# Eight half passes in a slot instead of four, tails moved to other products, and fewer small steps around them

## The chip, the cores and the metric

The kernel runs on one core of a Trainium2 chip. The time is the device time of one execution in microseconds (us). Three runs of the kernel before took 1652.21 us (median; 1650.31 to 1655.63).

## The reference

`x` is 2048 rows of 576 values. The kernel computes `x + s * g`, where both branches start from the same normed rows.

```python
xn = layernorm(x)                                    # [2048, 576]
# s: attention, 32 heads of 18, each row sees itself and the 255 rows before it
q, k, v = split(xn @ wqkv)                           # wqkv [576, 1728]
p = softmax(where(mask, q @ k.T * 18 ** -0.5, -1e9))
s = (p @ v) @ wo                                     # wo [576, 576]
# g: two branches multiplied, no nonlinearity between them
h = (xn @ w_gate) * (xn @ w_up)                      # [2048, 4608]
g = silu(h @ w_down)                                 # w_down [4608, 576]
out = x + s * g
```

## The kernel before

**Precision.** Every matrix is held as a sum of two f16 parts, a high one and a low one (what the rounding of the first left over). A product of two such matrices is three matmuls: high with high, high with low, low with high. One matmul of 128 rows of the contraction by 128 by 256 columns is called a pass here.

**Tiling of the gate and up products.** 4608 columns are worked off in 18 groups of 256 (`g`), 2048 rows of `x` in 4 chunks of 512 (`c`): 72 slots, and slot `sl` is group `sl // 4`, chunk `sl % 4`. In a slot the product of a 512-wide weight block (576 = 512 + 64 rows) with 512 rows of `x` is made by a seven-product scheme on 2 by 2 blocks: seven products `q` = 0 to 6 on sums and differences of blocks, in the order 0, 2, 1, 3, 4, 5, 6. Each has 12 passes (two kinds, gate and up; two blocks of 128; three part products). The differences of weights (`tw`) are formed per group by `t_sum`, `t_hi`, `t_lo`, the sums of `x` (`sx`, `xd`) once ahead.

**The last 64 rows.** 576 is not a multiple of 128: 64 rows are left. A tail is their product. A full tail pass carries 64 rows of two parts at once; what is left over is a half pass, a matmul with 64 rows of contraction, which uses half of the array's rows. In the kernel before, products 1, 4, 5 and 6 have tails: 1 and 6 with two full passes a kind, 4 and 5 with one full and one half (`seven_tail`, `seven_half`). A slot has 96 full passes and four half passes; the half passes stand together at place 11, those of product 4 on rows 0 to 63 of the array and those of 5 on rows 64 to 127, alternating.

**Banks.** The seven products use two PSUM banks (`up`, 512 columns: gate and up side by side). `ON` says which product accumulates on the bank of which: 1 on 0, 3 on 2, 5 on 3, 6 on 4. A product that goes on a bank that was already read out must wait for that reading. Readings (`seven_read`): product 0 and 1 by ScalarE (`seven_copy`), the others by VectorE (`seven_add`, one PSUM and one SBUF input), into f32 tiles `gt`. When a quarter is complete, `seven_mult` multiplies gate by up into `ht`; `h_hi` (ScalarE) and `h_lo` (VectorE) split that into two f16 parts `hh`.

**Down projection.** `down` n = 0 to 4 runs in the next slot: six passes of 512 columns each (n = 4: 24 passes of 64 columns) into one bank `dn`, and VectorE adds it to `acc`. The next `down` waits for that.

**Attention.** One step of two heads by 512 rows in each of slots 1 to 64: scores on TensorE (`score_pairs`, matmuls of 54 rows in pairs on the two halves of the array), masked row maximum on VectorE (`score`), exponent on ScalarE (`probs`), low part by a subtraction (`turn_probs`), then a DMA transpose into `pt`, then `weigh` on TensorE into `pv`; `finish` divides by the sum and adds the two parts, `finish2` splits the result.

**Order.** All is written out by hand: a slot has 16 places, `SEVEN_N` says how many passes each place issues, and the table `AT` gives the place of everything else (place 22 of a slot is place 6 of the next). At a place the passes come first, then scores, then `down`, then the rest. Each engine takes its instructions in this order; all DMAs go through the SP queue. Per group there is also the scaling of new weights: `ffn_raw` loads them, `ffn_amax` squares and sums, the maxima go out to DRAM and back (`ffn_spread_out`, `ffn_spread_in`), `ffn_scale` makes the powers of two on VectorE, `ffn_scale2` on GpSimd, then `up_hi`, `up_lo`, `dn_hi`, `dn_lo` split the weights.

Line numbers of the profile: L1116 full passes, L1072 and L1074 half passes, L991 `down`, L998 its addition, L908 `weigh`, L864 scores, L875 score reading, L1088 `seven_add`, L1084 `seven_copy`, L1094 `seven_mult`, L970 `h_hi`, L975 `h_lo`, L919 to L923 `finish`, L936 and L937 `finish2`, L896 `turn_probs`, L430 to L433 with L157 to L161 `ffn_scale`, L472 `t_sum`, L512 sums of `x`.

## Time and profile before

| what | value |
|---|---|
| median of 3 runs | 1652.21 us (1650.31 to 1655.63) |
| profiled execution, its own time | 1657.39 us |
| its span, first to last instruction | 1655.5 us |
| mean granted TensorE clock | 0.993 |
| busy: PE, DVE, ACT, POOL | 96%, 82%, 63%, 47% |
| first and last half pass | 191.1 us and 1582.6 us |

PE is TensorE's matmuls, PEld its weight loads, DVE is VectorE, ACT ScalarE, POOL GpSimd, SP the engine whose queue issues the DMAs. A row of the groups gives line, engine, operation, output and inputs, shapes and count, then busy us and mean ns of one, then the idle time before it and what ended that. Before 179 us lie the norm and the q, k, v products; slots 0 to 71 run from there to about 1588 us; the output projection ends the program. Matmuls are pipelined: the duration of one (some 270 ns) is longer than the distance to the next, so what a pass costs is read from the distance of starts.

### The profile page before, as it was taken

The page shows a single profiled execution, that of the slowest core. Times are in us where ns is not written, and L with a number is a line of the kernel's source. Part 1 is how long each engine was busy: PE and PEld are TensorE (multiplying, and loading weights), DVE is VectorE, ACT ScalarE, POOL GpSimd, SP SyncE. Part 2 cuts the span into 40 slices and gives each one's busy share as a digit, 9 for nine tenths or more (in the row PEclk, how much of TensorE's full clock was granted, in tenths as well). Part 3 has the DMA queues.
Part 4 walks back from the last instruction along what each step waited for, and adds up shares of the span by engine and source line. Part 5 has one row for each costly group of instructions (what it writes and reads, how often), then busy time and mean ns, then how long its engine had stood idle before and what let it go on. Part 6 is the DMA issues. An engine that isn't in the chain of part 4 may idle for free.

```text
span 1655.5 us, 40444 instructions
## 1 busy us (share of the span) xinstructions
PE 1584.0 (96%) x15498; PEld 1122.7 (68%) x15498; DVE 1353.2 (82%) x3049; ACT 1042.3 (63%) x1781; POOL 784.0 (47%) x993
## 2 busy tenths in 40 slices
PE   8999899999999999999999999999999999999898
PEld 5464566777766767676766666766676676677677
DVE  7536897989898979898988989898989797977654
ACT  6434566676677767777767676767777676752130
POOL 3125454546454746465655656464746473631000
PEclk9999999999999999999999999999999999999999
DMA  9562346475646777767868686768686868641228
GB/s 240 159 183 107 106 83 126 87 129 90 128 100 131 131 121 134 138 138 118 148 110 150 113 147 110 147 120 146 112 148 113 146 110 145 112 89 37 60 68 219
DMA packets 565745, 206.92 MB, mean 125 GB/s; under 512 B 506288, under 2 KB 546352, under 8 KB 565552
## 3 DMA queue, kind: packets, MB, share of 16 engines
q1 hardware_dynamic: 565552, 204.35, 63.9%
q8 instruction: 121, 1.98, 0.5%
q14 instruction: 72, 0.59, 0.1%
HBM read 76.63 MB, written 23.75 MB: 61 GB/s over the span
## 4 chain that ended last, share of the span: by engine, by line
PE 56%; DVE 23%; DMA 8%; issue 4%; SPq 4%; POOL 3%; ACT 1%; DVEq 0%; ACTq 0%; POOLq 0%
PE up L1116 23%; PE dn L991 14%; DMA pt<-pp 6%; PE s L373 3%; DVE gt L1088 3%; PE pv L908 3%; DVE acc L998 3%; DVE ht L1094 2%; DVE upw L185 2%; PE s L991 2%; DVE hh L975 2%; PE s L1223 2%; PE s L864 1%; PE up L1223 1%; PE up L373 1%
## 5 line engine op out<-in xcount | busy, mean ns | idle before, releaser
L991 PE MATMUL dn<-dnw,hh 128*128 128x512 f16 (+1 forms) x3168 | 448.9, 287 | 21.4 <-DVE acc L998 10.6
L1116 PEld LDWEIGHTS <-tw 128*128 128x128 f16 x3456 | 329.5, 98 | 78.0 <-issue 13.3
L991 PEld LDWEIGHTS <-hh 128*128 128x128 f16 x3456 | 224.6, 98 | 198.8 <-issue 37.6
L1116 PEld LDWEIGHTS <-upw 128*128 128x128 f16 x3456 | 322.6, 97 | 52.0 <-issue 0.4
L1116 PE MATMUL up<-XT,upw 128*128 128x256 f16 x2304 | 330.2, 272 | 0.0
L998 DVE SCALAR_TENSOR_TENSOR acc<-dn,sc,acc 128x512 f32<-128x512 f32 x310 | 214.7, 693 | 115.5 <-PE dn L991 110.2
L1088 DVE SCALAR_TENSOR_TENSOR gt<-up,gt 128x512 f32<-128x512 f32 x360 | 246.6, 685 | 31.5 <-PE up L1116 16.9
L1116 PE MATMUL up<-XT,tw 128*128 128x256 f16 x1728 | 237.4, 275 | 11.4 <-DVE gt L1088 11.4
L883 ACT ACTIVATE mx<-mx,sig 128x2 f32<-128x2 f32 x256 | 97.8, 382 | 218.7 <-DVE mx L875 218.7
L1116 PE MATMUL up<-sx,tw 128*128 128x256 f16 x1728 | 224.6, 273 | 0.4 <-DVE gt L1088 0.4
L908 PEld LDWEIGHTS <-pt 128*128 128x128 f16 x2880 | 107.8, 96 | 71.5 <-DMA pt<-pp 33.1
L970 ACT ACTIVATE hh<-ht 128x512 f16<-128x512 f32 x144 | 90.0, 625 | 91.0 <-DVE ht L1094 87.9
L908 PE MATMUL pv<-vt,pt 128*128 128x37 f16 x2880 | 123.8, 179 | 24.3 <-DMA pt<-pp 24.1
L1094 DVE TENSOR_TENSOR ht<-gt 128x256 f32<-128x256 f32 x288 | 147.0, 530 | 0.0
L1084 ACT ACTIVATE gt<-up 128x512 f32<-128x512 f32 x144 | 84.1, 584 | 56.5 <-PE up L1116 56.3
L1116 PE MATMUL up<-sx,upw 128*128 128x256 f16 x864 | 117.7, 273 | 0.0
L975 DVE SCALAR_TENSOR_TENSOR hh<-hh,ht 128x512 f16<-128x512 f16 x144 | 102.4, 711 | 0.1
L182 ACT ACTIVATE upw<-raw,sc 128x640 f16<-128x640 f32 x72 | 58.9, 820 | 54.1 <-DVE sc L161 50.2
L472 POOL TENSOR_TENSOR tf<-raw 128x256 f32<-128x256 f32 x102 | 74.2, 735 | 6.9 <-DVE sc L430 6.8
L301 ACT ACTIVATE upw<-raw 128x1280 bf16<-128x1280 f32 (+1 forms) x51 | 62.7, 1230 | 14.4 <-DMA raw<-in_B_w_up_dram 14.1
L185 DVE SCALAR_TENSOR_TENSOR upw<-raw,sc,upw 128x640 f16<-128x640 f32 x72 | 69.7, 969 | 0.0
L472 POOL TENSOR_TENSOR tf<-raw,tf 128x256 f32<-128x256 f32 x68 | 49.7, 731 | 35.3 <-DVE tw L185 35.3
(1288 smaller groups left out, 2744.1 us busy)
## 6 DMA issues: line engine op xcount, KB each, us to landing
raw<-in_B_w_down_dram SPq DMA_DIRECT2D x36, 288.0 KB
qk_d<-qp SPq DMA_DIRECT2D x18, 512.0 KB
raw<-in_B_w_gate_dram SPq DMA_DIRECT2D x36, 256.0 KB
raw<-in_B_w_up_dram SPq DMA_DIRECT2D x36, 256.0 KB
vt<-v_d SPq DMA_DIRECT2D x48, 111.0 KB
ks<-qk_d SPq DMA_DIRECT2D x96, 54.0 KB
v_d<-vo SPq DMA_DIRECT2D x16, 296.0 KB
xr<-in_A_x_dram SPq DMA_DIRECT2D x16, 288.0 KB
```

Of the source, the lines that this page charges most:

```text
L185: nc.vector.scalar_tensor_tensor(w, rv, s, h, op0=OP.mult, op1=OP.subtract)
L472: nc.gpsimd.tensor_tensor(t[:, to], x0, x1, op=OP.subtract)
L883: nc.scalar.activation(mx[:, 1], mx[:, 0], AF.Identity, bias=sig[:, 2:3], scale=sig[:, 1:2])
L908: nc.tensor.matmul(PVB[s][:, j, i, :VW], pt[:, nb * j + n + n // nb * nb], VT[s][:, lo_ + n % nb, j * VW:(j + 1) * VW], start=n == 0, stop ...
L970: nc.scalar.activation(hh[:, 0], h, AF.Copy, scale=1.0 / LO)
L975: nc.vector.scalar_tensor_tensor(hh[:, 1], hh[:, 0], -LO, h, op0=OP.mult, op1=OP.add)
L991: nc.tensor.matmul(to, a, b, start=q == 0, stop=q == len(l) - 1)
L998: nc.vector.scalar_tensor_tensor(d, src, SC[g][:, 9:10], d, op0=OP.mult, op1=OP.add)
L1084: nc.scalar.activation(seven_new(sl, name), CH[q], AF.Copy, scale=H_SC)
L1088: nc.vector.scalar_tensor_tensor(seven_new(sl, name), CH[q], H_SC, x, op0=OP.mult, op1=OP.add)
L1094: eng.tensor_tensor(HT[sl, f][:, 256 * i:256 * i + 256], u[:, 0:256], u[:, 256:512], op=OP.mult)
L1116: nc.tensor.matmul(CH[q][:, o], a, b, start=CH["first"], stop=last and q != 4, skip_group_check=q in ON)
```

## The change

What it does, part by part:

- **Tails.** Products 1, 2, 5 and 6 carry the tails, each with one full pass and one half pass a kind (`TAIL`, `seven_tail`). A slot has 92 full passes and eight half passes. These stand in two stretches of four: after product 1 at place 6 (products 1 and 2), and after product 5 at place 13 (products 6 and 5; those of 6 open its bank's second use ahead of its other passes). Product 2 is now read at place 6, not when its own 12 passes end.
- **A difference of weights.** Product 5's tail takes the difference of two weight blocks: `wd_sum` (GpSimd, 128x128), `wd_hi` (ScalarE), `wd_lo` (VectorE, 64 rows), per kind and group, kept in unused columns of `XT2`.
- **Gate times up** in two steps of 512 columns instead of four of 256 (`seven_mult`). The first (`gt0`) goes to GpSimd, the second (`gt1`) stays on VectorE. `gt` has two named tiles of twice the width, one buffer each, instead of a ring of four.
- **Attention's end.** The two parts are added first, in one reduction, then GpSimd multiplies by the reciprocal; before, VectorE multiplied all columns and reduced twice.
- **Scale.** `ffn_scale` has four steps instead of seven.
- **One of eight subtractions** of `turn_probs` (row block 2, first head) goes from GpSimd to VectorE.
- **Places.** Nearly every entry of `AT` and `SEVEN_N` is new.

```diff
-           "mult": {1: 1, 4: 5, 5: 1, 6: 1},
+           "mult": {1: 3, 4: 8, 5: 1, 6: 1},
-           "raw": (4, 8, 13, 15, -1, 0),
-           "scale": (23, 31, 35, 48),
+           "raw": (8, 13, 15, 16, -3, -1),
+           "scale": (20, 25, 35, 39),
...
     def ffn_scale(g):
...
-        bits = sc[:, 0:3].bitcast(mybir.dt.int32)
-        nc.vector.tensor_scalar(bits, bits, 1, None, op0=OP.logical_shift_right)
-        nc.vector.tensor_scalar(sc[:, 0:3], sc[:, 0:3], 2.0 ** 64, None, op0=OP.mult)
-        power(sc[:, 0:3], sc[:, 3:6], sc[:, 6:9], FTOP)
+        bits, p = sc[:, 0:3].bitcast(mybir.dt.int32), sc[:, 3:6]
+        nc.vector.tensor_scalar(bits, bits, 1, 0x7F800000, op0=OP.logical_shift_right, op1=OP.bitwise_and)
+        nc.vector.tensor_scalar(p, sc[:, 0:3], 2.0 ** 65 / FTOP, 2.0 * LEAST / FTOP, op0=OP.mult, op1=OP.max)
+        nc.vector.tensor_scalar(sc[:, 6:9].bitcast(mybir.dt.int32), p.bitcast(mybir.dt.int32), 0x7F800000, None,
+                                op0=OP.bitwise_xor)
...
+    def wd_part(g, kind, i):
+        o = 1024 * (g % 2) + 512 * i + 128 * kind
+        return XT2[:, o:o + 128]
+
+    def wd_sum(g, kind):
+        r = RAW[g, kind][:, 4]
+        nc.gpsimd.tensor_tensor(r[:, 0:128], r[:, 0:128], r[:, 128:256], op=OP.subtract)
+
+    def wd_hi(g, kind):
+        hi(wd_part(g, kind, 0), RAW[g, kind][:, 4, 0:128], SC[g][:, 6 + kind:7 + kind])
+
+    def wd_lo(g, kind):
+        h = slice(64, 128)
+        lo(wd_part(g, kind, 1)[h], RAW[g, kind][h, 4, 0:128], SC[g][h, 6 + kind:7 + kind], wd_part(g, kind, 0)[h])
...
     def finish(s):
...
-        nc.vector.reciprocal(rc, pv[:, :, :, 2 * DH:VW])
-        nc.vector.tensor_tensor(pv[:, :, :, 0:2 * DH], pv[:, :, :, 0:2 * DH], rc.to_broadcast([128, 2, 4, 2 * DH]),
-                                op=OP.mult)
-        for j in range(2):
-            nc.vector.tensor_reduce(o3[:, j], pv[:, j, :, 0:2 * DH].rearrange("p i (k d) -> p i d k", k=2),
-                                    axis=AX.X, op=OP.add)
+        nc.vector.reciprocal(rc, pw[:, :, 2 * DH:VW])
+        nc.vector.tensor_reduce(o3, pw[:, :, 0:2 * DH].rearrange("p n (k d) -> p n d k", k=2), axis=AX.X, op=OP.add)
...
     def finish2(s):
...
+        nc.gpsimd.tensor_tensor(o3, o3, RC.pop(s).to_broadcast([128, 8, DH]), op=OP.mult)
...
-    def seven_half(g, c):
+    def seven_half(g, c, pair, stop):
         for kind in range(2):
-            o = slice(256 * kind, 256 * kind + 256)
-            w, x, _ = seven_tail(g, c, 4, kind)
-            nc.tensor.matmul(a[:, o], w[0:64, 9], x[0:64], start=False, stop=kind == 1)
-            w, _, xh = seven_tail(g, c, 5, kind)
-            nc.tensor.matmul(b[:, o], w[64:128, 9], xh, start=False, stop=False, skip_group_check=True)
+            for q, s in zip(pair, stop):
+                _, _, w, x = seven_tail(g, c, q, kind)
+                nc.tensor.matmul(CH[q][:, 256 * kind:256 * kind + 256], w, x, start=False, stop=s and kind == 1,
+                                 skip_group_check=q in ON)
...
     def seven_place(sl, place):
...
-        if place == 11:
-            seven_half(g, c)
-            seven_read(sl, 4, place)
+        if place == STRETCH[0]:
+            seven_half(g, c, (1, 2), (True, True))
+            seven_read(sl, 2, place)
+            seven_read(sl, 1, place)
+        if place == STRETCH[1]:
+            seven_next(g, c)
+            seven_half(g, c, (6, 5), (False, True))
+            seven_read(sl, 5, place)
...
-    SEVEN_N = (4, 8, 7, 6, 5, 5, 6, 8, 3, 5, 3, 6, 7, 8, 8, 7)
+    SEVEN_N = (4, 8, 7, 6, 5, 5, 5, 4, 5, 5, 4, 6, 7, 7, 7, 7)
```

How the order moves, at three places. First TensorE, around the half passes of a slot in the middle. Before, they follow product 4's last full passes, and the scores (L864) follow them:

```order
L1116 MATMUL up_7101<-XT_83,upw_7041 128x256
L1072 LDWEIGHTS upw_6895
L1072 MATMUL up_7101<-XT_83,upw_6895 128x256
L1074 LDWEIGHTS upw_5851
L1074 MATMUL up_6949<-XT2_84,upw_5851 128x256
L1072 LDWEIGHTS upw_7041
L1072 MATMUL up_7101<-XT_83,upw_7041 128x256
L1074 LDWEIGHTS upw_6364
L1074 MATMUL up_6949<-XT2_84,upw_6364 128x256
L864 LDWEIGHTS qs_6754
L864 MATMUL s_7140<-ks_6593,qs_6754 128x384
```

In the change this is place 6: the half passes are L1104, the full ones L1151, the scores L889.

```order
L1151 MATMUL up_12220<-XT_83,upw_11693 128x256
L1104 LDWEIGHTS upw_11142
L1104 MATMUL up_12220<-XT_83,upw_11142 128x256
L1104 LDWEIGHTS upw_12214
L1104 MATMUL up_12270<-XT2_84,upw_12214 128x256
L1104 LDWEIGHTS upw_11693
L1104 MATMUL up_12220<-XT_83,upw_11693 128x256
L1104 LDWEIGHTS upw_12145
L1104 MATMUL up_12270<-XT2_84,upw_12145 128x256
L889 LDWEIGHTS qs_12055
L889 MATMUL s_12345<-ks_11957,qs_12055 128x384
```

The four half passes (first and second bank alternating: products 1 and 2) stand between full passes and scores as before. A second stretch like it stands at place 13, between product 5's passes and the slot's other four scores, which before had full passes ahead of them.

Second VectorE, at the new scale in slot 2 of a group. Before: product 2 read (L1088), the seven steps, the last `down`'s addition (L998), then score readings (L875).

```order
L1088 SCALAR_TENSOR_TENSOR gt_11724<-up_11705,gt_11700 128x512
L430 TENSOR_REDUCE sc_11731<-tf_11648 128x3
L432 TENSOR_SCALAR sc_11731<-sc_11731 128x3
L433 TENSOR_SCALAR sc_11731<-sc_11731 128x3
L157 TENSOR_SCALAR sc_11731<-sc_11731 128x3
L159 TENSOR_SCALAR sc_11731<-sc_11731 128x3
L160 RECIPROCAL sc_11731<-sc_11731 128x3
L161 TENSOR_SCALAR sc_11731<-sc_11731 128x3
L998 SCALAR_TENSOR_TENSOR acc_1850<-dn_11752,sc_10365,acc_1850 128x4x64
L875 ISA sm__11785,mx_11784<-s_11744,bias_1854 128x384
L875 ISA mx_11784 128x1
```

In the change the scale's four steps stand between `h_lo` of the first half (L999) and of the second, ahead of product 2's reading (L1121) and the first `down`'s addition (L1022); score readings are L900.

```order
L999 SCALAR_TENSOR_TENSOR hh_11536<-hh_11536,ht_11518 128x512
L432 TENSOR_REDUCE sc_11621<-tf_11415 128x3
L434 TENSOR_SCALAR sc_11621<-sc_11621 128x3
L435 TENSOR_SCALAR sc_11621<-sc_11621 128x3
L436 TENSOR_SCALAR sc_11621<-sc_11621 128x3
L999 SCALAR_TENSOR_TENSOR hh_11583<-hh_11583,ht_11543 128x512
L1121 SCALAR_TENSOR_TENSOR gt1_11658<-up_11585,gt0_11553 128x512
L1022 SCALAR_TENSOR_TENSOR acc_1854<-dn_11669,sc_10272,acc_1854 128x512
L900 ISA sm__11690,mx_11689<-s_11661,bias_1858 128x384
```

The addition that followed the scale directly now stands ahead of it, with the next one three instructions behind.

Third GpSimd, at the end of an attention step. Before: subtractions of `turn_probs` (L896), a difference of weights (L472), then `finish2` (L936, L937).

```order
L896 TENSOR_TENSOR pp_15985<-sm__15888,pp_15985 128x384 x2
L472 TENSOR_TENSOR tf_15904<-raw1_15394,tf_15904 128x256
L936 CAST ob_16026<-o3_16028 128x4x36
L937 TENSOR_TENSOR ob_16026<-o3_16028,ob_16026 128x4x36
L896 TENSOR_TENSOR pp_16083<-sm__16045,pp_16083 128x384 x2
```

In the change `finish2` (L953, L960, L961), a weight difference for the tail (L469) and then the gate times up product of the slot (L1126); L921 is `turn_probs`, L492 `t_sum`.

```order
L921 TENSOR_TENSOR pp_15806<-sm__15751,pp_15806 128x384 x2
L953 TENSOR_TENSOR o3_15857<-o3_15857,rc_15856 128x144
L960 CAST ob_15855<-o3_15857 128x4x36
L961 TENSOR_TENSOR ob_15855<-o3_15857,ob_15855 128x4x36
L469 TENSOR_TENSOR raw1_15255<-raw1_15255 128x128
L1126 TENSOR_TENSOR ht_15908<-gt0_15601 128x512
L492 TENSOR_TENSOR tf_15743<-raw1_15255 128x256
L921 TENSOR_TENSOR pp_15920<-sm__15885,pp_15920 128x384
```

The product stands behind all of `finish2` on this engine, and the next step's subtractions stand behind the product.

131 lines of the change are left out of this document (67 added, 64 removed), and 22 rows, old and new, of the table AT.

## The prediction

> **What bounds the kernel now.** The page comes first: PE is busy nearly all the time and leads the chain, with DVE behind it.
>
> ```profile
> PE 1584.0 (96%) x15498; PEld 1122.7 (68%) x15498; DVE 1353.2 (82%) x3049; ACT 1042.3 (63%) x1781; POOL 784.0 (47%) x993
> PE 56%; DVE 23%; DMA 8%; issue 4%; SPq 4%; POOL 3%; ACT 1%; DVEq 0%; ACTq 0%; POOLq 0%
> ```
>
> A busy PE need not be at its peak, so next comes the timeline of PE at the half passes of slot 31 and in the slot after (start, duration, what). Distances of starts give the prices.
>
> ```profile
> 794.88 0.38 PE L1116 MATMUL up<-XT,upw 128*128 128x256 f16 x2
> 795.20 0.28 PE L1072 MATMUL up<-XT,upw 64*128 64x256 f16 x1
> 795.20 0.28 PE L1074 MATMUL up<-XT,upw 64*128 64x256 f16 x1
> 795.32 0.27 PE L1072 MATMUL up<-XT,upw 64*128 64x256 f16 x1
> 795.32 0.27 PE L1074 MATMUL up<-XT,upw 64*128 64x256 f16 x1
> 795.43 0.49 PE L864 MATMUL s<-ks,qs 54*128 54x384 f16 x4
> 795.85 0.47 PE L908 MATMUL pv<-vt,pt 128*128 128x37 f16 x12
> ...
> 801.22 1.45 PE L991 MATMUL dn<-dnw,hh 128*128 128x512 f16 x6
> 802.51 0.46 PE L908 MATMUL pv<-vt,pt 128*128 128x37 f16 x12
> 802.81 1.03 PE L1116 MATMUL up<-XT,upw 128*128 128x256 f16 x8
> 803.68 0.27 PE L1116 MATMUL up<-sx,tw 128*128 128x256 f16 x1
> ```
>
> Eight full passes take 803.68 - 802.81 = 0.87 us, 0.109 each, with no air between them. Four half passes take 795.43 - 795.20 = 0.23 us: they start two at a time, so a pair costs about one full pass. Two full passes from 794.88 would end at 795.10, but the halves start at 795.20: a change of the array's row split costs 0.10 us.
>
> So while nothing holds it PE is at its own limit, and the slots differ by waits. The third view is the stretches: all attention slots, then slots 28 to 31, one group (us; busy us and count of PE, PEld, DVE, ACT, POOL; clock, DMA share, GB/s).
>
> ```profile
> 178.80:1454.00 1275.20, 1222.23 (x12833) 886.30 (x12832) 1121.87 (x2581) 908.12 (x1544) 708.38 (x885) 0.99 0.70 124
> 722.20:741.20 19.00, 19.00 (x207) 13.96 (x206) 18.46 (x44) 16.25 (x28) 9.87 (x13) 1.00 0.72 155
> 741.20:760.60 19.40, 19.02 (x207) 13.80 (x205) 14.41 (x37) 14.30 (x25) 8.08 (x10) 1.00 0.98 147
> 760.60:781.50 20.90, 19.20 (x207) 13.81 (x205) 18.45 (x43) 14.79 (x25) 11.89 (x15) 1.00 0.70 119
> 781.50:800.70 19.20, 18.97 (x206) 13.84 (x204) 18.86 (x41) 12.45 (x22) 15.30 (x18) 1.00 0.65 97
> ```
>
> In the attention slots PE is idle 1275.2 - 1222.2 = 53.0 us; a slot without a wait takes 19.0. DVE is full in the first and last slot of a group (18.46 of 19.00, 18.86 of 19.20), and the third loses 1.7. Fourth, what PE waits for over the program (total us, times, longest):
>
> ```profile
> PE pv L908 <- DMA pt<-pp: 24.1, 20, 2.6
> PE up L1116 <- DVE gt L1088: 11.8, 7, 5.7
> PE dn L991 <- DVE acc L998: 10.6, 25, 0.9
> PE dn L991 <- DVE hh L975: 9.5, 12, 0.8
> ```
>
> Two things can therefore be won: passes, and these waits. Attention's transposes arriving late cost 24.1, and DVE being late for `down` costs 20.1.
>
> **A, the passes.** A slot loses four full passes and gains four half passes in pairs: -4 x 0.109 + 0.23 = -0.205 us. Both stretches of half passes now stand against scores. In the rows above the split changes once ahead of halves and scores together, so the second stretch uses a change that the other four scores pay already. Over 64 attention slots that is -13.1 us. The eight slots without scores are different:
>
> ```profile
> 1507.92 0.27 PE L1074 MATMUL up<-XT,upw 64*128 64x256 f16 x1
> 1508.13 1.05 PE L1116 MATMUL up<-XT,tw 128*128 128x256 f16 x8
> ```
>
> From the second pair (1507.92) to the next full pass is 0.21 us, where 0.11 would do, so leaving costs 0.10 as well. A second stretch there costs 0.20 and wins 0.205: nothing. The Trainium skill (TensorEngine Tiling (Array Packing), Key Properties) says that switching the tiling mode drains the engine. The trace agrees, with 0.10 us each way; were every second stretch to pay both, it would take 0.20 x 64 = 12.8 us back and A would be nothing.
>
> **What DVE is relieved of**, which carries C.
>
> ```profile
> L1094 DVE TENSOR_TENSOR ht<-gt 128x256 f32<-128x256 f32 x288 | 147.0, 530 | 0.0
> L512 DVE TENSOR_TENSOR sx<-sx,XT 128x512 f32<-128x512 f32 x5 | 3.9, 784 | 0.5 <-POOL sx L512 0.4
> L923 DVE TENSOR_REDUCE o<-pv 128x72 f32<-128x144 f32 x128 | 33.4, 302 | 2.2
> L920 DVE TENSOR_TENSOR pv<-pv,rc 128x288 f32<-128x288 f32 x64 | 29.8, 466 | 2.2
> L157 DVE TENSOR_SCALAR sc<-sc 128x3 f32<-128x3 f32 x18 | 14.3, 794 | 0.6
> L159 DVE TENSOR_SCALAR sc<-sc 128x3 int32<-128x3 int32 x18 | 10.7, 596 | 0.6
> L161 DVE TENSOR_SCALAR sc<-sc 128x3 f32<-128x3 f32 x18 | 7.0, 386 | 0.6
> L512 POOL TENSOR_TENSOR sx<-sx,XT 128x512 f32<-128x512 f32 x11 | 13.3, 1210 | 27.5 <-DVE sx L516 23.9 <-DVE sx L512 3.2
> L937 POOL TENSOR_TENSOR ob<-o,ob 128x144 f16<-128x144 f32 x64 | 34.3, 535 | 5.1
> ```
>
> Per slot: four products of 256 columns become one of 512 (the other goes to POOL), 4 x 0.530 - 0.784 = -1.34. Attention's end loses the multiplication and has one reduction of 288 instead of two of 144. That reduction isn't shown; it costs between the multiplication of 288 (0.466) and two reductions (0.604), and I take 0.5: -0.57. One subtraction of 384 columns comes over from POOL, between the 0.530 of 256 and the 0.784 of 512, so 0.66. The scale loses `power`'s steps L157, L159 and L161 (1.78 together) and gets back one exclusive-or, no dearer than L159's 0.60: -1.18 a group, -0.30 a slot. Two `wd_lo` a group on 64 rows by 128 columns, nearest to the 144 columns of 0.302, add 0.15. Together -1.4 us of some 17.5 (70.2 in the four stretches). POOL gets the product (1.21), attention's multiplication (0.535) and the weight differences (two a group, under 0.3 a slot), and gives up one subtraction of about 0.9: +1.1 on 11.3. ACT gets two small splits a group. Neither becomes the bound.
>
> **B, the late transposes.** The waits lie in a group's first two slots, and the chain of waits (start, us, what) shows why:
>
> ```profile
> 742.37 0.38 SPq L177
> 744.65 4.61 DMA pt<-pp
> 749.31 0.47 PE pv L908 x12
> ```
>
> L177 are loads of the up weights. They stand in SP's queue at places 13 and 15, just ahead of the third row block's transpose (16), which then lands at 749.26 and is waited for. In the change the loads stand at 15 and 16 and that transpose at 19, so the queue is clear of them. But its use also moves, from 22 to 25, and the DMA engines still carry the same load bytes in that slot (DMA share 0.98 above). From subtraction to use it stays six places, 7 us at 19/16 = 1.19 a place, against 4.6 for the transpose. Ends: all of the 24.1 won, or none. I take 14, somewhat over half, because the order in the queue is mended and the traffic is not.
>
> **C, DVE late for `down`.** In slot 2 of a group the scale stands on DVE between product 2 and the last `down`'s addition, for which PE waits. In the change that addition is ahead of the scale, the scale is 1.2 us shorter, and DVE has 1.4 us less in every slot. Ends: the 20.1 all gone, or all still there; I take 12.
>
> **D, new waits.** Product 2 is now read at place 6, and product 3 goes on its bank right behind. PE's cover between them is four scores (795.85 - 795.43 = 0.42), one change (0.10), a `down` (802.51 - 801.22 = 1.29) and 12 small passes (0.30): 2.1 us. The reading takes:
>
> ```profile
> L1088 DVE SCALAR_TENSOR_TENSOR gt<-up,gt 128x512 f32<-128x512 f32 x360 | 246.6, 685 | 31.5 <-PE up L1116 16.9 <-PE up L1072 14.6
> ```
>
> So DVE may be 1.4 us late without harm. Between places 1 and 6 it has one subtraction, two `h_lo` and the additions, and it should be idle by then except behind the scale. A group's first slot also has two `t_lo` between the score readings, ahead of an addition that the next `down` needs. Ends: none, or 1.5 us in each of 16 groups, 24; I take 6.
>
> The prologue and the rest are costed at nothing. PE is full there under the q, k, v products, and the six new `wd` instructions lie on the other engines. If that cover fails, it costs their own time, about 3 us. The 5.7 us wait (the longest of L1088's) stays.
>
> **The sum**, against the profiled execution's 1657.39 (span 1655.5): -13.1 - 14 - 12 + 6 = -33, so 1624. The median of the runs, 1652.21, lies 5.2 below that execution, so 1619.
>
> **Rivals.** *Passes alone:* the waits keep their size because other DVE and DMA work moves with them. The 0.98 of DMA share speaks for it, the emptier DVE against it. That gives 1652 - 13 = 1639. The Trainium skill (SBUF — State Buffer, Who interferes with whom) would lead there: a DVE operation with two SBUF inputs and a GpSimd one that reads SBUF exclude each other for a whole instruction. This trace fits it with
>
> ```profile
> L1094 DVE TENSOR_TENSOR ht<-gt x288: 407/418/1141, 191.6 to 1590.0; 128x256 f32<-128x256 f32 x144
> ```
>
> 0.418 in the median and 1.141 at most. As a mechanism of this kernel: if DVE were held for the whole 1.21 of the new POOL product in each slot, its -1.4 would shrink to -0.2, and C with it; B would be left, 1652 - 13 - 14 + 6 = 1631 at best.
>
> *Slower, by the product on POOL:* it stands behind all of `finish2` there, and ACT's `h_hi` stands behind the product, with the exponents of row block 3 behind that on ACT. From that block's subtraction (place 20) to its use (27) are 7 places, 8.3 us; two subtractions (1.8) and the transpose (4.6) leave 1.9. Up to there POOL's lateness is free; beyond, each us costs PE one in every slot. POOL's own work (12.4 of 19) speaks against it. But POOL runs in order and waits for ACT's `pp`, 6.0 us at the longest:
>
> ```profile
> POOL pp L896 <- ACT pp L890: 449.4, 173, 6.0
> ```
>
> If it is 0.7 beyond that in 64 slots: 1619 + 45 = 1664.
>
> *It doesn't do what it says:* half passes that run one by one, 0.115 each, would cost 4 x 0.115 + 0.23 - 0.435 = +0.26 a slot instead of -0.205, 72 x 0.46 = 33 more than forecast: 1652. The rows of either stretch alternate between the array's halves and between two banks as they do now, so this is unlikely.
>
> *New waits at product 3:* D at its upper end and B at nothing: 1619 + 18 + 14 = 1651, no change.
>
> *Nearly all waits gone:* B and C at full size, D at nothing: 1619 - 10 - 8 - 6 = 1595.
>
> **How the numbers follow.** The forecast (1606 to 1634) has 0.45, nearly all waits gone (below 1606) 0.15, passes alone 0.18 with the lock in it, new waits at product 3 with half passes one by one 0.10, slower by POOL 0.12. What a measurement of this kernel can tell from no change is 0.3%, 5 us. Faster is 0.45 + 0.15 + 0.18 = 0.78, and 0.02 of the new waits: 0.80. Same is the other 0.08, slower 0.12. The range reaches from 1598 (leaving out a third of the case below 1606) to 1650 (leaving out POOL's case and a little of no change). The forecast's own range is 1606 to 1634.
>
> **What would show it.** A: half passes in pairs at two places, two starts within 0.01 us, and a slot without a wait of 18.8 instead of 19.0. B: PE's wait for `pt` at 10 or below in all. C: PE's waits for L998 and L975's successors at 8 or below, and DVE below 17 us a slot. D: a wait of product 3's first pass for `seven_add` behind place 6, at most 0.2 a slot on average. Wrong would be ACT's `h_hi` waiting for POOL by over 2 us in most slots, or PE idle for more than 50 us between the first slot and the last attention slot.

## The result and the profile after

The changed kernel takes 1642.51 us in the median of 5 runs (1640.25 to 1647.93); the kernel before, in runs beside it, took 1654.71 (1650.31 to 1655.63). The ratio is 0.9939, with a 95% interval of 0.9915 to 0.9964: 10 us faster, where 33 were forecast. The time lies in the predicted range, a long way above the forecast's own range.

The profiled run of the changed kernel took 1647.93 us, with a span of 1646.2: 9.3 us under the span before (1655.5). The stretch table places the difference (slots 0 to 19; slots 20 to 63; the rest, which begins with slot 64, the last with attention; the columns as in the prediction). Of the kernel before:

```profile
178.80:562.00 383.20, 366.11 (x3708) 266.50 (x3707) 337.37 (x782) 259.40 (x466) 203.55 (x272) 0.99 0.57 109
562.00:1439.60 877.60, 842.46 (x8978) 610.02 (x8977) 771.08 (x1772) 635.61 (x1057) 497.16 (x606) 1.00 0.75 130
1439.60:1655.50 215.90, 203.39 (x1844) 151.70 (x1842) 140.02 (x260) 60.45 (x98) 27.22 (x36) 0.98 0.40 96
```

The same three of the change:

```profile
178.80:551.00 372.20, 361.15 (x3715) 263.05 (x3714) 308.16 (x701) 264.05 (x474) 225.27 (x299) 0.99 0.58 112
551.00:1432.00 881.00, 840.86 (x8978) 601.17 (x8977) 715.91 (x1585) 646.75 (x1079) 551.65 (x672) 0.99 0.74 130
1432.00:1646.20 214.20, 202.83 (x1838) 148.11 (x1835) 132.78 (x232) 61.53 (x102) 38.93 (x48) 0.98 0.41 98
```

The gain of 11 us lies in the first 20 slots; the 44 later ones, two thirds of the attention stretch, take 3.4 us more than before. PE's idle time in the 64 slots is 17.1 + 35.1 = 52.2 us before and 11.0 + 40.1 = 51.2 after: in sum it has not shrunk. The prediction had named idle time above 50 us here as a sign of being wrong. Yet VectorE (third pair of numbers) did lose its work there: (771.08 - 715.91) / 44 = 1.25 us a slot, and GpSimd gained (551.65 - 497.16) / 44 = 1.24.

The slots themselves tell more. A slot is counted here from the start of its first 256-column pass to the next slot's; the means are over slots 20 to 63, 11 of each place in a group.

| place in the group | 0 | 1 | 2 | 3 | lightest slot |
|---|---|---|---|---|---|
| length before, us | 19.18 | 20.81 | 20.57 | 19.22 | 18.9 |
| length after | 21.36 | 20.00 | 19.85 | 18.89 | 18.65 |
| VectorE busy before | 18.51 | 14.48 | 18.27 | 18.84 | |
| VectorE busy after | 18.55 | 13.60 | 16.65 | 16.28 | |

Eleven groups gain 8.9 us in the second slot, 7.9 in the third and 3.6 in the fourth, and lose 24.0 in the first. VectorE became lighter in every place but the first, and there it is as busy as a slot without waits is long. (Two of VectorE's score readings, 0.55 us each, left the first slot for other slots in the change; without that it would be busier than before.)

What PE waits for over the program (total us, times, longest), after:

```profile
PE pv L933 <- DMA pt<-pp: 24.6, 26, 2.3
PE up L1151 <- ACT gt L1117: 11.8, 13, 1.4
PE dn L1015 <- DVE hh L999: 7.2, 16, 0.9
PE up L1151 <- DVE gt L1121: 7.1, 6, 5.2
PE dn L1015 <- DVE acc L1022: 2.1, 12, 0.2
```

The transposes are waited for as long as before (24.1), but elsewhere: before, nearly all of it was at row block 2's use; after, 20.2 us (21 times) are at row block 3's. Of the 20.1 us at `down` nothing is left where it was, in a group's third and fourth slot; the 7.2 at `h_lo` (16 times) and the 2.1 at the additions (12 times, 0.2 each) are new ones, in a group's first slot. The wait for ScalarE's reading of product 0 (L1117) is new too. Of the 7.1 us for VectorE's readings (L1121), 5.2 lie in slot 0.

The passes run as forecast. PE's timeline of the change at the second stretch of half passes:

```profile
783.77 0.38 PE L1151 MATMUL up<-XT,XT 128*128 128x256 f16 x2
784.09 0.28 PE L1104 MATMUL up<-xd,upw 64*128 64x256 f16 x1
784.09 0.28 PE L1104 MATMUL up<-XT 64*128 64x256 f16 x1
784.21 0.27 PE L1104 MATMUL up<-xd,upw 64*128 64x256 f16 x1
784.21 0.27 PE L1104 MATMUL up<-XT 64*128 64x256 f16 x1
784.32 0.49 PE L889 MATMUL s<-ks,qs 54*128 54x384 f16 x4
```

The half passes start in pairs, at 784.09 and 784.21, and the scores follow 0.11 after the second pair: the scores pay the change of the row split on leaving, as they did before.

**Why the transposes are still late.** The chain of waits in the first slot of the eighth group (start, us, what):

```profile
714.11 1.20 DVE pp L921
715.43 1.45 SPq L924
716.93 0.65 SPq L862
717.63 0.44 SPq L862
718.12 0.61 SPq L862
718.77 0.43 SPq L862
719.38 5.92 DMA pt<-pp
725.35 0.47 PE pv L933 x12
```

It is another row block than the one that the prediction looked at. SP issues row block 2's transpose (L924) at 715.43, then four loads of the next slot's keys (L862), and only then, at 719.2, is the queue free for row block 3's transpose, which lands at 725.3 with PE waiting. The kernel before has four such loads at the same point of its queue. There row block 2's transpose and the loads have place 16 and row block 3's subtraction place 19; in the change they have 19 and 20. So the loads, which before ended 0.5 and 1.6 us ahead of that subtraction in a group's second and third slot (means), now end 1.1 and 0.9 us behind it; in the first slot they end 1.8 behind it, before 1.3.

**What a group's first slot now waits for.** ScalarE, GpSimd and PE in that slot (timelines; in brackets the idle time before an instruction and what ended it):

```profile
711.05 0.82 ACT L184 ACTIVATE upw<-raw,sc 128x640 f16<-128x640 f32 x1
712.33 0.63 ACT L994 ACTIVATE hh<-ht 128x512 f16<-128x512 f32 x1 [0.45 <-POOL ht L1126]
712.86 0.58 ACT L1117 ACTIVATE gt<-up 128x512 f32<-128x512 f32 x1
```
```profile
710.33 0.73 POOL L492 TENSOR_TENSOR tf<-raw 128x256 f32<-128x256 f32 x1
711.02 1.27 POOL L1126 TENSOR_TENSOR ht<-gt 128x512 f32<-128x512 f32 x1
```
```profile
712.17 0.38 PE L1151 MATMUL up<-XT,upw 128*128 128x256 f16 x2
713.49 0.60 PE L1151 MATMUL up<-XT,upw 128*128 128x256 f16 x4 [0.94 <-ACT gt L1117]
```

GpSimd's product comes behind a weight sum (L492), `h_hi` waits for the product, ScalarE's reading of product 0 stands behind `h_hi`, and product 1, which goes onto the same bank, waits 0.94 us. A few us later VectorE is late for `h_lo` and the next reading.

### The profile page after: what moved, and what is told of

It reads as the page before. It is cut to its first block, busy times and chain, and to the rows that moved or that the text cites. A ratio compares the mean times of both kernels' runs of the same rounds, so it can differ in the third digit from the quotient of the medians.

```text
span 1646.2 us, 40284 instructions
## 1 busy us (share of the span) xinstructions
PE 1576.6 (96%) x15498; PEld 1106.7 (67%) x15498; DVE 1261.2 (77%) x2752; ACT 1060.2 (64%) x1817; POOL 875.5 (53%) x1100
## 4 chain that ended last, share of the span: by engine, by line
PE 47%; DMA 11%; DVE 11%; POOL 9%; issue 9%; ACT 7%; SPq 5%; ACTq 0%; POOLq 0%; DVEq 0%
PE up L1151 20%; PE dn L1015 10%; DMA pt<-pp 7%; POOL pp L921 4%; PE s L375 3%; PE s L1015 2%; ACT pp L915 2%; PE pv L933 2%; PE s L1254 2%; SPq L924 2%; DVE upw L187 2%; DVE acc L1022 2%; PE up L1254 1%; PE up L1104 1%; PE up L375 1%
## 5 line engine op out<-in xcount | busy, mean ns | idle before, releaser
L1151 PEld LDWEIGHTS <-tw 128*128 128x128 f16 x3456 | 317.7, 98 | 64.1 <-issue 10.2
L1151 PEld LDWEIGHTS <-upw 128*128 128x128 f16 x3024 | 285.0, 98 | 81.9 <-issue 35.2
L1121 DVE SCALAR_TENSOR_TENSOR gt<-up,gt 128x512 f32<-128x512 f32 x360 | 247.0, 686 | 99.3 <-PE up L1104 82.7
L1022 DVE SCALAR_TENSOR_TENSOR acc<-dn,sc,acc 128x512 f32<-128x512 f32 x310 | 214.8, 693 | 112.3 <-PE dn L1015 110.5
L1151 PE MATMUL up<-XT,upw 128*128 128x256 f16 x2016 | 253.7, 272 | 10.4 <-ACT gt L1117 10.4
L1151 PE MATMUL up<-XT,tw 128*128 128x256 f16 x1728 | 229.4, 277 | 5.9 <-DVE gt L1121 5.9
L1151 PE MATMUL up<-sx,tw 128*128 128x256 f16 x1728 | 231.4, 273 | 2.6 <-ACT gt L1117 1.4
L933 PEld LDWEIGHTS <-pt 128*128 128x128 f16 x2880 | 115.7, 96 | 67.5 <-DMA pt<-pp 45.0
L933 PE MATMUL pv<-vt,pt 128*128 128x37 f16 x2880 | 123.4, 179 | 24.8 <-DMA pt<-pp 24.6
L1126 POOL TENSOR_TENSOR ht<-gt 128x512 f32<-128x512 f32 x72 | 92.1, 1279 | 73.2 <-DVE gt L1121 73.1
L1151 PE MATMUL up<-sx,upw 128*128 128x256 f16 x864 | 119.0, 274 | 0.0
L999 DVE SCALAR_TENSOR_TENSOR hh<-hh,ht 128x512 f16<-128x512 f16 x144 | 99.5, 710 | 1.1
L1117 ACT ACTIVATE gt<-up 128x512 f32<-128x512 f32 x144 | 83.8, 582 | 25.4 <-PE up L1104 16.1
L492 POOL TENSOR_TENSOR tf<-raw 128x256 f32<-128x256 f32 x102 | 82.1, 805 | 3.9 <-DVE sc L432 3.3
L1126 DVE TENSOR_TENSOR ht<-gt 128x512 f32<-128x512 f32 x72 | 74.6, 1036 | 0.2
L187 DVE SCALAR_TENSOR_TENSOR tw<-tf,sc,tw 128x512 f16<-128x512 f32 x68 | 52.9, 799 | 15.7 <-ACT tw L184 15.7
```

Of the source, the lines that this page charges most:

```text
L187: nc.vector.scalar_tensor_tensor(w, rv, s, h, op0=OP.mult, op1=OP.subtract)
L492: nc.gpsimd.tensor_tensor(t[:, to], x0, x1, op=OP.subtract)
L933: nc.tensor.matmul(PVB[s][:, j, i, :VW], pt[:, nb * j + n + n // nb * nb], VT[s][:, lo_ + n % nb, j * VW:(j + 1) * VW], start=n == 0, stop ...
L999: nc.vector.scalar_tensor_tensor(hh[:, 1], hh[:, 0], -LO, h, op0=OP.mult, op1=OP.add)
L1022: nc.vector.scalar_tensor_tensor(d, src, SC[g][:, 9:10], d, op0=OP.mult, op1=OP.add)
L1117: nc.scalar.activation(seven_new(sl, name), CH[q], AF.Copy, scale=H_SC)
```

## The experiments

Medians in us; the ratio is to the kernel before, run beside each (its medians there were 1644 to 1655), so kernels that ran beside different runs of it are compared by ratios; that median alone moved by 11 us. The base is the change unless another is named. The new theory is that B failed by the queue, and that D is a first slot short of VectorE and ScalarE time; the rival is that single pieces in the way cause each wait.

### The late transposes

Three runs on row block 3's transpose: its use one place later; the loads behind it in the queue; both.

```diff
-                 (13, 14, 15, 18, 25), (13, 14, 15, 19, 25), (15, 17, 18, 20, 27), (15, 17, 18, 20, 27)),
+                 (13, 14, 15, 18, 25), (13, 14, 15, 19, 25), (15, 17, 18, 20, 28), (15, 17, 18, 20, 28)),
...
-           "end": (28, 30, 33),
+           "end": (29, 30, 33),
```

The second (x2) is one number, and x8 has both edits.

```diff
-           "load": (3, 8, 10),
+           "load": (5, 8, 10),
```

> The change, with row block 3's use of its transposed probabilities at place 28 instead of 27, and attention's end one place later (29). Theory: the wait for transposes was not won because it moved from row block 2 (now 1.5 to 2.4 us early) to row block 3 (0.05 early in the median); one place, 1.2 us, takes PE's waits for pt from 24.6 to about 10 us and the time from 1642 to about 1629. Rival, the DMA engines' traffic sets when transposes land and the wait goes to wherever the next use is: waits for pt stay above 20, time 1640 to 1645.

> The change, with the next step's loads of k two places later (5 instead of 3), so that they no longer stand in SP's queue between the transposes of row blocks 2 and 3. Theory that the queue order delays block 3: its issue comes up to 1.2 us earlier in three of four slots, waits for pt from 24.6 to about 14, time about 1633. Rival, that block 3 is late by what comes before its subtraction (ScalarE in order, then GpSimd): issue follows the subtraction sooner, but waits for pt fall by less than 4, time 1639 to 1645.

> The change with both: loads of k two places later and row block 3 used one place later. If both work on the same wait, as the theory has it, they don't add up: waits for pt from 5.6 to about 3, time 1622 to 1627. If each takes away a wait of its own, -16 twice: about 1611.

| run | time | ratio, 95% interval | wait for `pt` |
|---|---|---|---|
| the change | 1642.51 | 0.9939, 0.9915 to 0.9964 | 24.6 |
| x1, use a place later | 1626.86 | 0.9868, 0.9831 to 0.9905 | 10.7 |
| x2, loads behind the transposes | 1626.34 | 0.9867, 0.9830 to 0.9904 | 5.6 |
| x8, both | 1630.65 | 0.9875, 0.9843 to 0.9908 | 11.0 |

PE's waits in x2:

```profile
PE up L1151 <- ACT gt L1117: 17.7, 23, 1.3
PE dn L1015 <- DVE hh L999: 7.2, 16, 0.9
PE pv L933 <- DMA pt<-pp: 5.6, 10, 1.4
```

Either edit alone wins about the 14 us that the prediction gave term B (12 by the ratios, 16 by the medians), and both together no more: it is one wait. It was lost by one place, or by four loads too close in front of one transpose.

### The first slot: moving pieces

x3 puts GpSimd's product back on VectorE:

```diff
-           "eng": (0, 1, 0, 0, 0, 0, 0, 0, 0, 0, 1, 0, 0, 0),
+           "eng": (1, 1, 0, 0, 0, 0, 0, 0, 0, 0, 1, 0, 0, 0),
```

x4 moves ScalarE's split of the third up weights ahead of the product and the difference of weights behind it:

```diff
-           "up_hi": (37, 38, 63, 60),
-           "up_lo": (42, 40, 65, 62),
-           "wd": ((58, 46), (65, 65), (67, 66)),
+           "up_hi": (37, 38, 61, 60),
+           "up_lo": (42, 40, 64, 62),
+           "wd": ((58, 46), (67, 68), (69, 70)),
```

x6, on x2, moves GpSimd's last weight sum behind its product:

```diff
-           "sum": ((30, 36, 42, 60, 63), (38, 43, 50, 60, 62)),
+           "sum": ((30, 36, 42, 60, 63), (38, 43, 50, 60, 63)),
```

x7, on x2, moves VectorE's part of the difference of weights five places later:

```diff
-           "wd": ((58, 46), (65, 65), (67, 66)),
+           "wd": ((58, 46), (65, 65), (72, 72)),
```

> The change, with both gate times up products on VectorE (none on GpSimd). Theory that GpSimd's product is what delays h_hi and, on ScalarE behind it, row block 3 and product 0's reading: waits for product 0's reading (11.8 us) under 4, waits for pt under 12, time about 1628. Rival, that ScalarE's own queue in a group's first slot does it and VectorE has no room: those waits stay, and VectorE (0.7 to 1.0 us more in each slot) gives 5 to 15 us more waits at down; time 1645 to 1655.

> The change, with the weight work of a group's first slot spread: the third up split two places earlier (61, low part 64), the tail's difference split two to four places later (67 and 68, low parts 69 and 70). Theory that this work, in order on ScalarE and VectorE, causes the first slot's waits (product 0's reading 11.8, h_lo 7.2 us): both fall to under half, time about 1632. Rival, that the GpSimd product ahead of h_hi causes them: they stay within 3 us, time 1639 to 1645.

> The kernel with the later loads of k (1626 us), and one weight difference of a group's last slot a place later (63), so that GpSimd makes the gate times up product 0.73 us sooner there. Theory: GpSimd's product, behind weight differences, holds h_hi and, behind that on ScalarE, the reading of product 0 in a group's first slot: PE's waits for that reading (17.7 us there) fall by 0.5 to 0.7 in 16 groups, to about 8, time about 1617; the first slot from 20.9 to about 20.2. Rival, ScalarE's own work is what is late: first slot 20.9, time 1624 to 1628.

> The kernel with the later loads of k (1626 us), and the low parts of the tail's weight difference at place 72 instead of 67 and 66, behind h_lo on VectorE; the high parts stay at 65. Theory: in a group's first slot h_lo is late by VectorE's extra work, 0.7 us of it these two: PE's waits for h_lo at down (7.2 us) go, time about 1618, first slot about 20.3. Rival, that VectorE's work is only moved and the next addition for down is late instead, or SP is held by the weight loads that wait for these: time 1624 to 1634.

| run | time | ratio | PE's largest waits in a group's first slot |
|---|---|---|---|
| x3 | 1643.49 | 0.9974, 0.9950 to 0.9998 | `h_lo` 21.0, VectorE's readings 15.9 |
| x4 | 1658.64 | 1.0064, 1.0041 to 1.0087 | VectorE's readings 40.5 |
| x6 | 1627.91 | 0.9864, 0.9834 to 0.9893 | `h_lo` 20.4, reading of product 0 5.1 |
| x7 | 1622.59 | 0.9839, 0.9813 to 0.9865 | VectorE's readings 15.9, product 0 13.0 |

In x3, x6 and x7 the wait that was aimed at went, as the theory of single pieces expects, and each time another came up. (In each row 5.2 us of VectorE's readings lie in slot 0.) x3 shows what GpSimd's product does: without it there the wait for product 0's reading is gone, and that for the transposes is 6.5 us, with the loads where the change has them; VectorE, with the product, is then late instead. The transposes wait less in x4 too (9.4), where PE loses more elsewhere in the first slot, so how much of x3's 6.5 is the product's doing is not shown. In x6 the reading of product 0 costs 5.1 instead of 17.7, and this row comes in its place:

```profile
PE dn L1015 <- DVE hh L999: 20.4, 32, 1.6
```

x4 failed outright, and the wait for product 0's reading stayed at 9.4 of 11.8. VectorE stood at the difference of weights waiting for ScalarE, so product 2 was read late and product 3's first pass waited. That is the prediction's rival "new waits at product 3", found in a variant and not in the change:

```profile
PE up L1151 <- DVE gt L1121: 40.5, 22, 5.2
```

### The first slot: how much, and of what

Four runs on x2. x9 has the difference of weights wholly in the fourth slot of the group before:

```diff
-           "wd": ((58, 46), (65, 65), (67, 66)),
+           "wd": ((47, 46), (49, 50), (51, 52)),
```

x10 has that and x6's edit of `sum`; x11 has the edits of x6 and x7 together. x12 leaves the difference of weights out from the third group on, which makes part of the output another number:

```diff
         for f, p in zip((wd_sum, wd_hi, wd_lo), AT["wd"]):
-            for kind in range(2):
+            for kind in range(2 if g < 2 else 0):
                 at(b, p[kind], f, g, kind)
```

> The version with the loads of the next slot behind the last transposes (place 5), and in it all six instructions of the difference of weights moved from a group's first slot (places 65 to 67) into the fourth slot of the group before (sums at 47 and 46, ScalarE's splits at 49 and 50, VectorE's at 51 and 52), where no other weight work stands. Nothing is left out. Theory 'a group's first slot is short of ScalarE and VectorE time': two splits of 0.34 us leave ScalarE and two leave VectorE there, so PE's waits for the reading of product 0 (17.7 us in the version with the loads moved) and for h_lo (7.2) fall to under 10 together, the first slot from 20.9 to about 20.0 us, 16 groups: 10 to 14 us less, about 1614 (ratio to the kernel before 0.976 to 0.981). Rival 'the place of single pieces does not matter, the wait goes to the next reading': waits for VectorE's readings of products 3 and on come up by as much, 1622 to 1628 (0.984 to 0.988).

> As the run with the difference of weights in the fourth slot, and GpSimd's last weight sum of the second kind one place later (62 to 63), behind GpSimd's product of the gated halves. Theory 'ScalarE is held by h_hi, which waits for GpSimd's product': the wait for product 0's reading goes (from 17.7 in the version with only the loads moved to about 5, as when this sum was moved alone), and as VectorE has no difference of weights in its way any more, no wait for h_lo takes its place (20.4 us then): 1608 to 1614 (0.972 to 0.978). Rival 'first slot short of time altogether': as the run without the later sum, within 4 us.

> The version with the loads moved to place 5, GpSimd's last weight sum at 63 instead of 62, and VectorE's part of the difference of weights at place 72 instead of 67 and 66. Each of the two moves alone took one of two waits of PE away and brought up another. Theory 'two separate waits, each with its own piece': both early waits (readings of product 0, h_lo) stay under 6 us each and a wait for VectorE's reading of product 3 of 10 to 16 us is left: 1612 to 1618 (0.977 to 0.981). Rival 'one shortage that moves': 1622 to 1628 (0.984 to 0.988), with the wait for VectorE's readings above 20 us.

> The version with the loads moved to place 5, with the difference of weights (its sum on GpSimd, split on ScalarE, rest on VectorE) left out from the third group on: product 5 then uses the weights' difference of an older group, so that part of the output is another number, and the time is that of the kernel without this work. It sizes what the six added instructions a group cost wherever they stand. Theory 'they cost the first slot its waits': first slot 20.9 to 19.6 us or less, 14 groups, 12 to 20 us less: 1606 to 1614 (0.972 to 0.979). Rival 'the waits come from the new order of products and readings, not from this work': within 4 us of 1626 (0.985 to 0.988), with the waits for product 0's reading (17.7) as they were.

| run | time | ratio | slot lengths by place | VectorE busy by place |
|---|---|---|---|---|
| x2 | 1626.34 | 0.9867, 0.9830 to 0.9904 | 20.92 19.59 18.97 18.68 | 18.69 13.59 16.56 16.03 |
| x9 | 1627.57 | 0.9883, 0.9840 to 0.9925 | 20.27 19.12 19.07 19.69 | 17.88 13.57 16.61 18.13 |
| x10 | 1625.38 | 0.9874, 0.9838 to 0.9911 | 19.84 19.63 19.19 19.68 | 17.71 13.58 16.64 18.09 |
| x11 | 1614.81 | 0.9809, 0.9774 to 0.9844 | 20.76 19.00 19.30 18.68 | 19.53 13.58 16.61 16.03 |
| x12 | 1610.37 | 0.9784, 0.9747 to 0.9821 | 20.28 19.08 18.86 18.68 | 17.88 13.58 16.60 16.11 |

x12 sizes the work: the six instructions a group cost 14 (by the ratios) to 16 us of x2's time, and the two intervals do not meet. But the first slot falls only to 20.28, where the theory had 19.6 or less, and the wait for product 0's reading is 14.8 us of x2's 17.7, 0.94 in each of the later first slots, as the rival had it. So this work is the cause of `h_lo`'s wait (7.2, now gone) and of longer early first slots (20.06 against 18.59), and not of that wait, which x3 and x6 tie to GpSimd's product and the weight sum ahead of it. x9, which came out as its rival, shows that the six are not merely in a bad place: its first slot is as short as x12's, but in the fourth slot they lengthen it by 1.0 us and fill VectorE to 18.1, and PE's wait comes up there; the stretch of the four slots of the eighth group in x9, first and fourth:

```profile
709.40:729.60 20.20, 19.04 (x206) 13.74 (x204) 17.80 (x37) 16.17 (x28) 13.89 (x18) 1.00 0.76 144
767.10:786.80 19.70, 18.83 (x206) 13.81 (x205) 18.14 (x39) 13.33 (x24) 15.21 (x15) 1.00 0.56 112
```

x10, with that weight sum moved as well, has the shortest first slot (19.84) and pays in the same place; its time is the rival's.

x11 went as the theory of two separate pieces said (its interval and x2's overlap by a hair), but not only for its reason. Its gain over x2 is half in the first 20 slots (366.2 us against 372.8), whose rows of scores are shorter: there a first slot falls from 20.06 to 18.27, no wait left. In the later ones it stays at 20.7, with VectorE busy for all but 1.2 us of it:

```profile
698.70:719.50 20.80, 19.44 (x207) 13.78 (x206) 19.57 (x39) 16.79 (x30) 14.44 (x18) 1.00 0.72 143
719.50:738.10 18.60, 18.60 (x206) 13.66 (x204) 13.52 (x33) 14.38 (x25) 7.62 (x11) 1.00 0.65 152
```

So both theories hold, each in its part: where scores are short the pieces were in the way and can be moved; where they are full x11's first slot is short of VectorE time, which moving within it does not mend. VectorE is not the only limit there, though: in x12 it has 2.4 us left in the first slot, and ScalarE's reading of product 0 still comes late. The second slot, one row down, has 5 us of VectorE to spare.

### Two more on the shortage

Three runs on x11. x14 has the up weights' split two places earlier:

```diff
-           "up_hi": (37, 38, 63, 60),
+           "up_hi": (37, 38, 61, 60),
```

x15 gives attention's subtraction back to GpSimd, and x16 has both edits.

```diff
-           "eng": (0, 1, 0, 0, 0, 0, 0, 0, 0, 0, 1, 0, 0, 0),
+           "eng": (0, 1, 0, 0, 0, 0, 0, 0, 0, 0, 0, 0, 0, 0),
```

> The version with the loads at place 5, the last weight sum at 63 and VectorE's part of the difference of weights at 72 (1614.8 us), with ScalarE's split of the third up weights two places earlier (63 to 61), where ScalarE has 2.3 us idle. Theory 'this 0.82 us split holds the reading of product 0': the wait for product 0's reading falls from 9.0 to about 3, 1606 to 1610 (0.976 to 0.979). Rival 'VectorE, which is behind by then, sets the slot': the wait for the readings of product 3 (14.8) grows by as much, 1612 to 1617 (0.980 to 0.983).

> The same version with attention's subtraction of row block 2, first half, given back from VectorE to GpSimd in every slot: VectorE has 1.0 to 1.2 us less a slot, GpSimd about 1.0 more, on 12 of 19. Theory 'VectorE is short in every slot': the wait for product 3's reading (14.8) and the addition's 4 us go, 1603 to 1609 (0.974 to 0.978). Rival 'GpSimd's product and h_hi behind it set ScalarE': GpSimd is late, the wait for product 0's reading grows and transposes of row block 2 come late, 1616 to 1630 (0.982 to 0.990).

> The same version with both: the split at 61 and the subtraction on GpSimd. If the two causes are separate they add: 1596 to 1604 (0.970 to 0.975). If there is one shortage that both relieve, as the better one of the two within 3 us.

The times are 1615.19 (ratio 0.9807, 0.9754 to 0.9859), 1617.33 (0.9810, 0.9755 to 0.9864) and 1615.72 (0.9810, 0.9761 to 0.9859): the same as x11, all three. x14 takes the wait for product 0's reading from 9.0 to 5.5 and wins nothing, because the next wait, for VectorE's reading, stays at 14.8; that is near its rival, in which this wait would have grown. In x15 that wait falls to 8.9 and the late transposes come back, since GpSimd's subtraction is late for them (it ends 1.5 us later in a group's fourth slot, and 11.6 us of the waits are at row block 2's use in the first slot behind it):

```profile
PE pv L933 <- DMA pt<-pp: 16.5, 21, 2.3
```

In x15 VectorE is hardly lighter in the first slot (19.10 us against 19.53), although a subtraction of over a us was taken from it: what is left there takes longer. That is told below.

### The passes, and the scale

x5 (on the change) and x17 (on x11) move the second pair of scores one place forward, so that the second stretch of half passes stands between full passes:

```diff
-           "pairs": (6, 13),
+           "pairs": (6, 12),
```

x13 (on the change) and x18 (on x11) put the scale's seven steps back, at the new places:

```diff
-        bits, p = sc[:, 0:3].bitcast(mybir.dt.int32), sc[:, 3:6]
-        nc.vector.tensor_scalar(bits, bits, 1, 0x7F800000, op0=OP.logical_shift_right, op1=OP.bitwise_and)
...
+        bits = sc[:, 0:3].bitcast(mybir.dt.int32)
+        nc.vector.tensor_scalar(bits, bits, 1, None, op0=OP.logical_shift_right)
+        nc.vector.tensor_scalar(sc[:, 0:3], sc[:, 0:3], 2.0 ** 64, None, op0=OP.mult)
+        power(sc[:, 0:3], sc[:, 3:6], sc[:, 6:9], FTOP)
```

> The change, with the second four scores at place 12 instead of 13, so that the second stretch of half passes stands between full passes. Theory: the stretch then pays its own two changes of the row split, 0.20 us in each of 64 slots: 12.8 us more, time about 1655 where the change took 1642; the lightest slots of attention go from 18.65 to 18.85. Rival, that a change of split costs nothing beside other work: 1642, slots of 18.65.

> The 1614.8 us version (loads at place 5, last weight sum at 63, VectorE's part of the difference of weights at 72) with the second pair of score products one place earlier (13 to 12), so that it no longer stands against the second stretch of half passes, which then pays its own two changes of the row split. Theory 'A is real time': 0.21 us in each of 64 attention slots, 13 us more, and as the transposes wait only 5.8 us there they can give back no more than that: 1622 to 1629 (ratio to the kernel before 0.984 to 0.989). Rival 'the scores' earlier place is worth as much': 1612 to 1618 (0.978 to 0.982).

> The changed kernel with one part undone: the scale of the up weights in its old seven steps of VectorE instead of four, at its new places. Theory 'term C came from the shorter scale': VectorE has 1.2 us more in a group's third slot, PE waits again for h_lo and the addition there (about 10 us over 16 groups), so 1648 to 1654 where the changed kernel has 1642.5 (ratio to the kernel before 0.998 to 1.002). Rival 'C came from the new order, the down addition ahead of the scale': no wait there, the same time within 4 us (0.991 to 0.996).

> The 1614.8 us version with the scale of the up weights in its old seven steps. Theory 'the longer scale only moved the late transposes in x13': here they hardly wait, so the longer scale brings nothing; the same to 4 us longer, 1613 to 1619 (0.979 to 0.983). Rival 'a longer scale helps by itself': 1604 to 1610 (0.974 to 0.978). If the shorter scale is worth what the prediction gave it, 1620 to 1626 (0.983 to 0.987).

x5 takes 1641.11 (0.9948, 0.9927 to 0.9970), no other time than the change, though its lightest slot is 18.86 instead of 18.65: the scores being earlier, the wait for the transposes fell from 24.6 to 15.4 and can have paid for most of it. x17 takes 1623.57 (0.9868, 0.9843 to 0.9893), against x11's 0.9809 some 9 us more (8.4 more than x18, which ran beside it and is told below). Where the transposes have nothing left to give, A shows in the time. The stretch in x17:

```profile
778.06 0.38 PE L1151 MATMUL up<-XT,XT 128*128 128x256 f16 x2
778.50 0.27 PE L1104 MATMUL up<-XT 64*128 64x256 f16 x1
778.70 0.94 PE L1151 MATMUL up<-sx,upw 128*128 128x256 f16 x7
```

From the second pair to the next full pass 0.20 us, where 0.11 did with scores behind.

x13 takes 1633.12 (0.9911, 0.9883 to 0.9939): not slower than the change, and if anything faster, which neither theory had. x18 takes 1615.21 (0.9825, 0.9801 to 0.9849), x11's time. The third slot of a group has no wait for `down` in x13 either. So the shorter scale is not what cured C. That leaves the new order, with the scale away from that addition, and VectorE's lighter third slot (18.27 us before, 17.46 in x13, 16.65 in the change); no run took these two apart. x13's own lead over the change (intervals overlap) goes with a shorter wait for transposes, 18.5 instead of 24.6, and with none where these hardly wait, in x18; that it is their timing is inferred.

## Why the prediction was right or wrong

**A, the passes (-13.1): right in mechanism, a little high in time.** Pairs in two places, no change to pay at the second; the lightest slot is shorter by 0.21 (first 16 slots) to 0.25. x17 gives about 9 of the 13 back when it is undone. The rule of the Trainium skill that was weighed against it (TensorEngine Tiling (Array Packing), Key Properties) would have cost A its gain, had the second stretch paid for a change both ways. It did not, since scores follow, at 0.11 us like one more pair; in x17, where none do, the changes cost the 9 us.

**What VectorE is relieved of (-1.4 a slot): right on the mean, wrong where it mattered.** It was 1.25 on the mean, and GpSimd's +1.1 was 1.24. But the sum was spread evenly over the slots of a group. In the first slot it was nothing (18.51 to 18.55). There (summed durations of a slot, means of the 11 later ones) the products give 1.91 - 1.38 = 0.53 and attention's end 0.67, while the subtraction takes 1.27 (not 0.66) and the difference of weights 2 x 0.352 = 0.70: +0.8 in all, which the two score readings that left the slot make up for. The scale's gain lies in another slot. That is the step that failed behind D.

**B (-14): wrong, nothing won.** The step that failed is "the queue is clear of them". For row block 2 the wait did go. But its transpose and the four loads behind it came down to place 19, one place ahead of row block 3's subtraction (20, before 19), whose way to its use (27) became 7 places instead of 8. The prediction looked at that block under "Slower, by the product on POOL", and found 1.9 us to spare; it left out the four loads in the queue, which take 2.3 (716.93 to 719.2 above). One place (x1) or the loads' place (x2) gives the 14 us.

**C (-12): right, larger than taken.** The 20.1 us went wholly from where they were, rather than 12 of them. Of the three reasons given, "the scale is 1.2 us shorter" was not needed (x13); "that addition is ahead of the scale" and the lighter VectorE are left, and which of them did it is open.

**D (+6): undersized, and the step that turned the sum.** It looked for a wait at product 3 behind product 2's reading and at `t_lo`, with 24 us as its upper end. In the attention slots of the change there is no such wait (x4 shows that it is one step away); one of 5.2 us is in slot 0, where 3.2 was lost before. ("The 5.7 us wait stays" did not hold: it was in slot 70, where 0.7 is left.) The price was paid at the bank that was not examined: product 1 behind ScalarE's reading of product 0, behind `h_hi`, behind GpSimd's product; and at `h_lo`. PE's new waits, nearly all in first slots, come to 22 us (11.8, 7.2, 2.1, and four of 0.3 at VectorE's readings) in place of 6; the 11 later first slots are 24 us longer, late transposes included, while the four early ones (20.06 each) take in sum what they took before. "Two `wd_lo` a group" were priced as 0.15 us a slot, and "ACT gets two small splits a group. Neither becomes the bound" was an average over a group as well; x12 prices that work alone at 14 to 16 us. With these sizes the sum comes close to the measured 10: -13 + 0 - 20 + 22 = -11.

**The rivals.** "Passes alone" (1639) was nearest in time, and in sum its waits kept their size (52.2 us of idle time and 51.2). That is partly luck: place by place C was won in full, B not at all, and D took the difference. "Slower by the product on POOL" named the right engines, `h_hi` behind GpSimd's product:

```profile
ACT hh L994 <- POOL ht L1126: 72.2, 22, 11.2
```

The long ones of these waits lie in the last six slots, without attention; in the attention slots there are 15, of 0.4 to 1.7 us, 8.8 together and 12 of them in first slots. The rival placed the harm at the exponents and the transposes of every slot; what x3 undoes for certain is a reading on the same engine, once a group.

In sum, the forecast of 1619 is reached by the change with three small corrections (x11, 1614.81, the fastest kernel here that computes everything, 0.9809 of the time before). The change as it stands has the passes and C, has not B, and pays D.

## What to carry to other kernels

When work moves off an engine, cost it for each stage of the cycle and not on the mean: the stage that was full may be the one that gains nothing and gets the new work. When a late transfer is mended, look at the next one in the same queue, what stands between the two, and its distance from producer to use. A wait that moves from one instruction to another as pieces are shifted can be a shortage in that stage, of one engine or of two; take work out, or spread it to a stage that has time.
